# A recurrence with two expert layers on one core: the bonus moves onto the diagonal of the scores, the state products go into 64-row quarters, and the first product takes tokens as its stationary operand

## The chip, the cores and the metric

The kernel runs on one core of a Trainium2 chip. The metric is the device time of one execution in microseconds (us). The inputs lie in the chip's main memory, `w_in` and `w_out` of the first layer as float64, the others as float32, and the float32 output is written there.

## The reference

Three parts follow one another. The first is a recurrence over time for 4 batches of 8 heads, 768 steps, head size 48. The second and the third are layers on the 3072 tokens that it gives, each a vector of 384.

```python
# recurrence, per batch and head; u is the bonus of the present step
for t in range(S):
    cur = outer(u * k[t], v[t])
    y[t] = r[t] @ (state + cur)
    state = w[t][:, None] * state + outer(k[t], v[t])
# first layer: x is y as [3072, 384]
h = x @ w_in                    # [3072, 2048]
g = h * cos(h)
x = g @ w_out                   # [3072, 384]
# second layer: 8 experts with 4 slots each
logits = x @ phi                # [3072, 32]
slots = softmax(logits, over tokens).T @ x
slot_out = relu(slots @ w1[e]) @ w2[e]      # for each expert e
out = softmax(logits, over slots) @ slot_out
```

## The kernel before

The recurrence is cut into 24 blocks `j` of 128 tokens (six to a batch), and each block into two chunks `c` of 64. Within a chunk the decays become running products by two scans on VectorE (`scan`, `sp`; lines 156 and 164), and the recurrence becomes small products for four pairs of heads. Step `A` (line 208) gives the scores of each chunk, key by query. Step `mask` (line 222) multiplies them by a strict triangle of ones, from PSUM into the tile `L`. The other half of `L` holds the decayed `r` (step `L`, line 187). Step `U` (line 259) adds up the chunk's own contribution to the state, `st` and `z` (lines 277 and 269) carry the state on, and `y` (line 288) multiplies `L` by a tile `rzs` that holds both the state and `v`.

The bonus `u` of the present step goes another way. `ru` on GpSimd (lines 169 and 170) multiplies `r`, `u` and `k`, `bo` on VectorE (line 243) sums that over a head, `bv` on GpSimd (line 251) multiplies the sum by `v`, and `yb` (line 297) adds it to `y` in PSUM with three transposing matmuls. From block 8 on (`WIDE = 8`) the matmuls of `A` take all 128 rows, half of them zeros, for which GpSimd clears half of `L` (`zl`, line 193). In `U` the operand `vz` has `v` of chunk 0 in its upper 64 rows and of chunk 1 in its lower, side by side with zeros, so that one matmul gives both chunks (96 columns).

The first layer works in 12 groups `g` of 256 tokens and 8 pairs `i` of 128 features each. `h` (lines 462 to 464) has weights as the stationary operand (`lhsT`) and tokens as the moving one, 18 matmuls of 256 columns for a pair, since both are split into a rounded and a remaining part. `turns`, `rest`, `cos` and `mul` (lines 474, 478, 482, 486) make `g` out of it on ScalarE and VectorE in turn. `l` (line 507) makes logits from `g`, `gT` and `gc` (lines 494, 499) turn `g` so that tokens lie on partitions, and `E` (line 603) sums up the slots from that. The product with `w_out` is folded into `phi` and into the slots; at the start the weights are decoded to float32 from the 64-bit words of the float64 inputs, on ScalarE and VectorE (`raw`, `abs`, `mx`, `d1`, `d2a`, `d2b`; lines 338 to 374), and `w_in` is split into its two parts (`whi`, `wn`, `wc`; line 405 is the second half of `wn`).

The order is written out by hand. A string `HEAD` lists some 2,000 steps with their block or group, and each engine takes its instructions in that order. All DMAs are issued from SP. Transposes, `A`, `U`, `y`, `wn` and some others get their PSUM from one pool `ps_a` of three banks, `h` from a pool of two.

Of the kernel before, what the change touches and what calls it, by code (L numbers as in the profile page):

```python
# [21 lines left out]
def rwkv_moe_kernel(ctx: ExitStack, tc: tile.TileContext, r, k, v, w, u, w_in, w_out, phi, w1, w2, cst, out):  # L22
# [7 lines left out]
    C = 64  # L30
# [6 lines left out]
    NBK = MF // 2  # L37
# [5 lines left out]
    WIDE = 8  # L43
# [10 lines left out]
    g_p = b_stack.enter_context(tc.tile_pool(name="g", bufs=4, side="right"))  # L54
    gt_p = b_stack.enter_context(tc.tile_pool(name="gt", bufs=12, side="right"))
# [35 lines left out]
    vz = [nat.tile([128, H, 2, D], F32, name=f"vz{i}") for i in range(2)]  # L91
# [14 lines left out]
    vn_t, rz_t, l_t, ks_t, ksn_t, q_t, bv_t, z_t = ({} for _ in range(8))  # L106
# [60 lines left out]
    def e_ru(j):  # L167
# [3 lines left out]
        bv_t[j] = ru  # L171
# [30 lines left out]
    def e_A(j):  # L202
        ks, L = ks_t[j], l_t[j]
# [68 lines left out]
    def e_rz(j, c):  # L272
        for a in range(2):
            nc.scalar.copy(rz_t[j][64 * a:64 * a + 64, c, :, a, RZ[a]], z_t[j, c][64 * a:64 * a + 64])  # L274

    def e_st(j, c):
        nc.vector.tensor_tensor(out=st_state, in0=pend["U", j][:, :, c, :], in1=z_t[j, c], op=ALU.add)

    def e_y(j):

        L, rz = l_t.pop(j), rz_t.pop(j)
        ps = tps(f"y{j}")[:, 0:DM].rearrange("p (c t) -> p c t", c=KD)
        begun = set()
# [66 lines left out]
    def e_abs(x, n, hf=None):  # L350
        if not hf:
# [94 lines left out]
    LAST = (NG - 1, NBK - 1)  # L446

    def b_h(g, i, mm):
        if mm == 0:
            pool, tag = (ps_a, "a") if NBK * g + i >= ATT else (ps_h, "h")  # L450
            hp = pool.tile([128, 2, G], F32, tag=tag, name=f"h{g}_{i}")
            h_t[g, i] = [hp[:, 0], hp[:, 1], hp]
        elif (g, i) == LAST:
            h_t[g, i][1] = ps_t.tile([128, 2, G], F32, tag="t", name=f"h{g}_{i}b")[:, 0]
        hp = h_t[g, i][mm]
        xh, xl = xh_t[g], xl_t[g]
        m = 2 * i + mm
# [611 lines left out]
```

## Time and profile before

| | |
|---|---|
| time, median of 3 runs | 543.63 us (542.59 to 544.12) |
| profiled execution: span from first to last instruction | 542.5 us |
| TensorE (PE) busy | 502.9 us, 93% |
| VectorE (DVE) busy | 435.2 us, 80% |
| ScalarE (ACT) busy | 310.7 us, 57% |
| GpSimd (POOL) busy | 125.4 us, 23% |
| mean granted TensorE clock | 0.98 of full speed |

The span is taken from one execution by the profiler; what lies around it (1.1 us to the median) is start and end of the program. Busy time is an average over stages with different limits, and matmuls overlap, so PE's busy time is no sum of their durations.

### The profile page before, as it was taken

How to read it: one execution, taken by the hardware profiler on the slowest of the kernel's cores; microseconds unless marked ns; L12 is line 12 of the kernel's file. 1: busy time of each engine (PE TensorE's matmuls, PEld its weight loads, DVE VectorE, ACT ScalarE, POOL GpSimd, SP SyncE). 2: the span in 40 equal slices, each digit the busy share in tenths (PEclk: the TensorE clock that was granted, in tenths of full speed). 3: DMA queues.
4: the chain of work that ended last, by engine and by line, in shares of the span. 5: the costliest groups of instructions: out<-in, count | busy, mean ns of one | idle time of the engine just before them, and what ended most of it. 6: DMA issues, size and time to landing. Idle time of an engine off the chain costs nothing.

```text
span 542.5 us, 16245 instructions
## 1 busy us (share of the span) xinstructions
PE 502.9 (93%) x6850; PEld 436.4 (80%) x6850; DVE 435.2 (80%) x826; ACT 310.7 (57%) x655; POOL 125.4 (23%) x163
## 2 busy tenths in 40 slices
PE   2769879989999999999999999999999999998994
PEld 1547668879898898999988989989998989894673
DVE  4999998998889879887879788989878877666423
ACT  3356567646747555676555665755657646666421
POOL 4520120254044213221420331352033100000400
PEclk9977998999999999999999999999999999999998
DMA  9994656444332432421440442065031565188958
GB/s 218 258 238 105 176 115 183 125 76 75 74 59 46 76 59 50 79 37 30 76 74 1 75 89 45 17 111 83 16 61 31 229 252 220 29 322 311 403 181 272
DMA packets 146713, 67.52 MB, mean 124 GB/s; under 512 B 127569, under 2 KB 134737, under 8 KB 146641
## 3 DMA queue, kind: packets, MB, share of 16 engines
q1 hardware_dynamic: 146640, 66.49, 48.4%
q8 instruction: 54, 0.88, 0.7%
q14 instruction: 19, 0.15, 0.1%
HBM read 61.75 MB, written 4.72 MB: 123 GB/s over the span
## 4 chain that ended last, share of the span: by engine, by line
PE 67%; DVE 18%; ACT 5%; DMA 4%; issue 2%; SPq 2%; DVEq 0%; ACTq 0%
PE h L462 10%; PE h L464 10%; PE h L463 10%; PE gT L494 6%; PE l L507 4%; PE E L603 3%; PE A L208 3%; PE y L288 3%; PE U L259 2%; DMA vz<-in_v_dram 2%; PE hps L797 2%; DMA rawi<-in_moe_w_in_dram 2%; PE so L837 2%; DVE L L222 2%; DVE pt L164 2%
## 5 line engine op out<-in xcount | busy, mean ns | idle before, releaser
L462 PE MATMUL h<-x,wu 128*128 128x256 f32 x573 | 171.5, 299 | 1.4 <-DVE g L486 1.3
L464 PE MATMUL h<-x,wu 128*128 128x256 f32 x573 | 160.9, 281 | 0.0
L463 PE MATMUL h<-x,wu 128*128 128x256 f32 x573 | 160.8, 281 | 0.0
L462 PEld LDWEIGHTS h<-x,wu 128*128 128x128 f32 x573 | 108.7, 190 | 3.6 <-DVE g L486 1.7
L463 PEld LDWEIGHTS h<-x,wu 128*128 128x128 f32 x573 | 108.8, 190 | 0.2
L464 PEld LDWEIGHTS h<-x,wu 128*128 128x128 f32 x573 | 108.5, 189 | 0.0
L482 ACT ACTIVATE g<-g,half_pi 128x512 f32<-128x512 f32 (+1 forms) x97 | 69.4, 719 | 44.7 <-DVE g L478 43.7
L486 DVE TENSOR_TENSOR g<-g,h 128x512 f32<-128x512 f32 x96 | 64.8, 677 | 26.7 <-ACT g L482 26.1
L474 ACT ACTIVATE g<-h 128x512 int32<-128x512 f32 x96 | 57.1, 596 | 42.0 <-PE h L464 32.6
L478 DVE SCALAR_TENSOR_TENSOR g<-g,h 128x512 f32<-128x512 int32 x96 | 65.0, 678 | 14.9 <-ACT g L474 13.9
L251 POOL TENSOR_TENSOR bv<-vz,bo 64x384 f32<-64x384 f32 x48 | 43.8, 914 | 139.5 <-DVE bo L243 54.6
L499 ACT COPY gt<-gT 128x512 f32<-128x512 f32 x89 | 51.6, 584 | 28.7 <-PE gT L494 28.1
L494 PE MATMUL gT<-cs,g 128*128 128x128 f32 x384 | 58.1, 275 | 0.3 <-ACT gt L499 0.2
L494 PEld LDWEIGHTS gT<-cs,g 128*128 128x128 f32 x384 | 43.7, 140 | 6.0 <-issue 3.7
L169 POOL TENSOR_TENSOR ru<-rn,u_b 128x384 f32<-128x384 f32 x24 | 27.5, 1145 | 57.2 <-issue 19.5
L193 POOL MEMSET L<- 64x512 f32 x32 | 16.6, 520 | 96.0 <-PE y L288 81.5
L156 DVE TENSOR_TENSOR_SCAN qt<-wf,one_b 128x520 f32<-128x520 f32 x24 | 30.6, 1275 | 7.3 <-ACT wf L151 7.3
L222 DVE TENSOR_TENSOR L<-A,cs 64x512 f32<-64x512 f32 x48 | 33.0, 688 | 4.0 <-PE A L208 2.9
L274 ACT COPY rzs<-z 64x192 f32<-64x192 f32 x96 | 33.4, 348 | 3.6 <-DVE z L269 2.6
L187 DVE TENSOR_TENSOR L<-rT,pt 64x512 f32<-64x512 f32 x48 | 32.9, 686 | 1.6 <-PE rT L141 0.6
L164 DVE TENSOR_TENSOR_SCAN pt<-wf,ini_f 128x520 f32<-128x520 f32 x24 | 31.7, 1320 | 0.1
L208 PE MATMUL A<-L,ks 128*64 128x64 f32 (+1 forms) x768 | 27.7, 223 | 3.2 <-DVE ks L199 2.1
(172 smaller groups left out, 837.8 us busy)
## 6 DMA issues: line engine op xcount, KB each, us to landing
we<-in_moe_w_dram SPq DMA_DIRECT2D x16, 1536.0 KB, 10.4
rawi<-in_moe_w_in_dram SPq DMA_DIRECT2D x7, 768.0 KB, 5.5
wn<-in_w_dram SPq DMA_DIRECT2D x24, 192.0 KB, 4.0
kn<-in_k_dram SPq DMA_DIRECT2D x24, 192.0 KB, 4.0
rn<-in_r_dram SPq DMA_DIRECT2D x24, 192.0 KB, 3.8
vz<-in_v_dram SPq DMA_DIRECT2D x48, 96.0 KB, 3.1
rzs<-in_v_dram SPq DMA_DIRECT2D x96, 48.0 KB, 2.8
out_dram<-ob SPq DMA_DIRECT2D x17, 256.0 KB, 3.6
```

The costliest lines, as they stand in the source:

```text
L208: nc.tensor.matmul(ps[64 - 64 * a:128 - 64 * a, s, :], lhsT=ks[k, s, :], rhs=L[k, a, s, :], start=True, stop=True)
L222: nc.vector.tensor_tensor(out=L[h, a], in0=ps[h], in1=mask[h].unsqueeze(1).to_broadcast([64, NS, C]), op=ALU.mult)
L251: nc.gpsimd.tensor_tensor(out=bv[h], in0=vn_t[j][h, :, c, :], in1=bo[h].to_broadcast([64, H, D]), op=ALU.mult)
L462: nc.tensor.matmul(hp, lhsT=wh, rhs=xh[:, c, :], start=(c == 0), stop=False)
L463: nc.tensor.matmul(hp, lhsT=wh, rhs=xl[:, c, :], start=False, stop=False)
L464: nc.tensor.matmul(hp, lhsT=wl, rhs=xh[:, c, :], start=False, stop=(c == KD - 1))
L474: nc.scalar.activation(gt.bitcast(I32), hp, AF.Copy, bias=0.25, scale=1.0 / TWO_PI)
L478: nc.vector.scalar_tensor_tensor(out=gt, in0=gt.bitcast(I32), scalar=-TWO_PI, in1=hp, op0=ALU.mult, op1=ALU.add)
L482: nc.scalar.activation(gt, gt, AF.Sin, bias=half_pi[:, 0:1])
L486: nc.vector.tensor_tensor(out=gt, in0=gt, in1=hp, op=ALU.mult)
L494: nc.tensor.transpose(ps[:, tt, mm, :], gt[:, mm, tt * 128:(tt + 1) * 128], ident)
L499: (nc.vector.tensor_copy if NBK * g + i >= ATT and i in (1, 2, 5) else nc.scalar.copy)(t, pend.pop(("gT", g, i)))
```

## The change

The bonus sum is written onto the diagonal of the scores. `bo` writes its sums beside each other, a new step `bs` copies the half that belongs to other partitions (two small copies on ScalarE), and a new step `D` on GpSimd writes the diagonal with zeros elsewhere into the scores' half of the tile (`affine_select`, two of 64x512 a block). `mask` then copies the scores over it only where the triangle is one (`copy_predicated` on VectorE). `bv`, `yb`, `zl` and their tiles are gone, and `A` takes 64 rows in every block. `U` is made of 16 matmuls of 48 columns in place of 8 of 96, each with 64 rows and 64 columns of the array, chunk 0 and chunk 1 into PSUM banks of their own; `v` comes by one DMA a block, not two.

In the first layer `x` becomes the stationary operand and the weights the moving one: 9 matmuls of 512 columns for 128 tokens and 512 features (`b_h`), 96 times. So `g` has tokens on partitions. `E` reads `g` itself (512 columns a matmul), `l` reads the turned copy (128 columns a matmul, 384 of them in place of 192 of 256). The pool of `g` grows from 4 to 13 buffers, that of the turned copies shrinks from 12 to 3. `HEAD` is a new list.

```diff
-    NBK = MF // 2
+    NBK = 4
+    NGB = 13
-    WIDE = 8
...
-    g_p = b_stack.enter_context(tc.tile_pool(name="g", bufs=4, side="right"))
-    gt_p = b_stack.enter_context(tc.tile_pool(name="gt", bufs=12, side="right"))
+    g_p = b_stack.enter_context(tc.tile_pool(name="g", bufs=NGB, side="right"))
+    gt_p = b_stack.enter_context(tc.tile_pool(name="gt", bufs=16 - NGB, side="right"))
...
     def e_A(j):
...
-                k = slice(0, 128) if j >= WIDE else slice(64 * a, 64 * a + 64)
+                k = slice(64 * a, 64 * a + 64)
...
-    def e_mask(j):
-        L, ps = l_t[j], pend.pop(("A", j))
+    def e_D(j):
+
         for a in range(2):
             h = slice(64 - 64 * a, 128 - 64 * a)
-            nc.vector.tensor_tensor(out=L[h, a], in0=ps[h], in1=mask[h].unsqueeze(1).to_broadcast([64, NS, C]), op=ALU.mult)
+            nc.gpsimd.affine_select(out=lt[j % 2][h, a], in_=bo_t[j][h, a].unsqueeze(2).to_broadcast([64, NS, C]),
+                                    pattern=[[0, NS], [-1, C]], compare_op=ALU.is_equal, fill=0.0, base=0, channel_multiplier=1)
+
+    def e_mask(j):
+        ps = pend.pop(("A", j))
+        for a in range(2):
+            h = slice(64 - 64 * a, 128 - 64 * a)
+            nc.vector.copy_predicated(out=lt[j % 2][h, a], mask=mask[h].bitcast(U32).unsqueeze(1).to_broadcast([64, NS, C]), data=ps[h])
...
+    def e_bs(j):
+        bo = bo_t[j]
+        for a in range(2):
+            nc.scalar.copy(bo[64 - 64 * a:128 - 64 * a, a, a::2], bo[64 * a:64 * a + 64, a, 1 - a::2])
...
     def e_U(j):
-        ksn, vn = ksn_t.pop(j), vn_t[j]
-        ps = tps(f"U{j}")[:, 0:2 * HP * D].rearrange("p (s c d) -> p s c d", c=2, d=D)
+        ksn = ksn_t.pop(j)
+        ps = [tps(f"U{j}_{c}")[:, 0:HP * D].rearrange("p (s d) -> p s d", d=D) for c in range(2)]
         for p in range(HP):
             for a in range(2):
-                nc.tensor.matmul(ps[64 * a:64 * a + 64, p], lhsT=ksn[:, p * 128 + 64 * a:p * 128 + 64 * a + 64],
-                                 rhs=vn[:, 2 * p + a], start=True, stop=True)
+                for c in range(2):
+                    h = slice(64 * c, 64 * c + 64)
+                    nc.tensor.matmul(ps[c][64 * a:64 * a + 64, p], lhsT=ksn[h, p * 128 + 64 * a:p * 128 + 64 * a + 64], rhs=vn[j % 2][h, 2 * p + a], start=True, stop=True)
...
-    def e_yb(j):
-
-        y = bv_t.pop(j).rearrange("p h d -> p (h d)")
-        for c in range(KD):
-            nc.tensor.matmul(pend["xT", j][:, c, :], lhsT=y[:, c * 128:(c + 1) * 128], rhs=ident, is_transpose=True,
-                             start=False, stop=c == KD - 1, skip_group_check=True)
...
+        o = (t % 2) * TB
+        xh, xl = (x[:, :, o:o + TB] for x in (xh_t[t // 2], xl_t[t // 2]))
+        for half, f in zip(h_t[t, q], cols):
+            for c in range(KD):
+                wh, wl = wu[q][:, 0, c, f], wu[q][:, 1, c, f]
+                nc.tensor.matmul(half[:, f], lhsT=xh[:, c, :], rhs=wh, start=(c == 0), stop=False)
+                nc.tensor.matmul(half[:, f], lhsT=xl[:, c, :], rhs=wh, start=False, stop=False)
+                nc.tensor.matmul(half[:, f], lhsT=xh[:, c, :], rhs=wl, start=False, stop=(c == KD - 1))
...
-            nc.tensor.matmul(lps_t[g][32 * mm:32 * mm + 32, 0:G], lhsT=p_sb[:, m, :], rhs=g_t[g, m // 2][:, m % 2, :],
-                             start=(m < 4), stop=(m >= MF - 4))
+            nc.tensor.matmul(lps_t[g][32 * m:32 * m + 32, o:o + TB], lhsT=p_sb[:, 4 * q + m, :], rhs=gt[:, m * 128:(m + 1) * 128],
+                             start=first, stop=False, skip_group_check=True)
...
-                                 rhs=gt_t[g, 4 * hf + q][:, tt, :], start=(tt == 0), stop=(tt == 1))
+                nc.tensor.matmul(ps[32 * q:32 * q + 32, cols], lhsT=dt_[:, tt, :], rhs=g_t[2 * g + tt, q][:, cols], start=(tt == 0), stop=(tt == 1))
```

The order of the instructions shows at three places what moved. A row has the line, the operation, output and inputs with their buffers, the output's shape and a count. The first place is TensorE at block 13, before the change: `U` and the scores `A` of the block, two steps of `l`, and `y` with the bonus product of the block before.

```order
L259 MATMUL U_3710<-vz_124,ksn_3642 64x96 x8
L208 MATMUL A_3719<-L_3689,ks_3590 64x64 x16
L507 MATMUL l_3499<-g_4_3619,p_sb 32x256 x2
L507 MATMUL l_3499<-g_5_3565,p_sb 32x256 x2
L288 MATMUL y_3747<-L_3330,rzs_125 32x64 x32
L297 MATMUL y_3747<-cs,bv_3413 128x128 x3
```

After the change, at block 14, `A` is followed by 16 matmuls of `U`, by turns into its two banks. Here are the last two of them and what comes behind.

```order
L239 MATMUL U_0_3766<-vn_123,ksn_3728 64x48
L239 MATMUL U_1_3767<-vn_123,ksn_3728 64x48
L468 MATMUL gT_2_3806<-cs,g_2_3726 128x128 x4
L434 MATMUL h_0_3811<-wu_345,x_3054 128x512
L435 MATMUL h_0_3811<-wu_345,x_3054 128x512
L436 MATMUL h_0_3811<-wu_345,x_3054 128x512
```

Between `U` and the next step that needs a bank of `ps_a` now stand a transposition of `g` and a product `h`; line 297 is gone. The second place is GpSimd at the first two blocks, before the change: `ru` for both, then `bv` for both.

```order
L169 TENSOR_TENSOR ru_201<-rn_117,u_b 128x384
L170 TENSOR_TENSOR ru_201<-ru_201,kn_119 128x384
L169 TENSOR_TENSOR ru_249<-rn_118,u_b 128x384
L170 TENSOR_TENSOR ru_249<-ru_249,kn_120 128x384
L251 TENSOR_TENSOR bv_354<-vz_123,bo_238 64x384 x2
L251 TENSOR_TENSOR bv_487<-vz_124,bo_288 64x384 x2
```

After the change the diagonal of a block stands behind its own `ru` and ahead of the next block's.

```order
L162 TENSOR_TENSOR ru_195<-rn_117,u_b 128x384
L163 TENSOR_TENSOR ru_195<-ru_195,kn_119 128x384
L207 AFFINE_SELECT lt_125<-bo_217 64x512 x2
L162 TENSOR_TENSOR ru_282<-rn_118,u_b 128x384
L163 TENSOR_TENSOR ru_282<-ru_282,kn_120 128x384
L207 AFFINE_SELECT lt_126<-bo_303 64x512 x2
```

So GpSimd reaches `ru` of block 1 only when `D` of block 0 has had its sums. The third place is VectorE at block 0, before the change, from the sum `bo` of block 0 to that of block 1.

```order
L243 TENSOR_REDUCE bo_238<-ru_201 128x8
L160 RECIPROCAL ini_f<-qt_215 128x8
L366 SCALAR_TENSOR_TENSOR ai_187<-rawi_185,ai_187 128x3x128
L164 SCALAR_TENSOR_TENSOR pt_247<-wf,ini_f 128x520
L187 TENSOR_TENSOR L_254<-rT_226,pt_247 64x512 x2
L222 TENSOR_TENSOR L_196<-A_264,cs 64x512 x2
L243 TENSOR_REDUCE bo_288<-ru_249 128x8
```

After the change, from `L` of block 0 to the masked copy and `ks` of block 1.

```order
L178 TENSOR_TENSOR lt_125<-rT_179,pt_192 64x512 x2
L225 TENSOR_REDUCE bo_217<-ru_195 128x2x4
L149 SCALAR_TENSOR_TENSOR qt_243<-wf,one_b 128x520
L256 TENSOR_TENSOR st_state<-U_0_223,z_0_163 128x192
L153 RECIPROCAL ini_f<-qt_243 128x8
L248 TENSOR_TENSOR z_1_273<-st_state,qt_189 128x192
L214 COPY_PREDICATED lt_125<-cs,A_246 64x512 x2
L184 TENSOR_TENSOR ks_280<-kT_268,qt_243 128x512
```

The masked copy of block 0 stands five instructions behind the sum `bo` of that block, on which it now depends by way of ScalarE and GpSimd; before, nothing on VectorE waited for that sum.

## Rows read from the trace of the kernel before

**Rows 1.** Page of the profile, part 1: busy us, share of the span, instructions of each engine.

```profile
PE 502.9 (93%) x6850; PEld 436.4 (80%) x6850; DVE 435.2 (80%) x826; ACT 310.7 (57%) x655; POOL 125.4 (23%) x163
```

**Rows 2.** Stretch, length, busy us of PE, PEld, DVE, ACT, POOL (xinstructions), PEclk, DMA share, GB/s.

```profile
0.00:120.00 120.00, 93.14 (x1078) 74.72 (x1079) 107.85 (x166) 66.41 (x128) 32.30 (x48) 0.93 0.73 169
120.00:490.00 370.00, 365.80 (x5085) 331.94 (x5083) 306.67 (x610) 224.45 (x478) 86.43 (x106) 1.00 0.37 85
490.00:543.00 53.00, 43.92 (x689) 29.73 (x689) 20.71 (x52) 19.86 (x50) 6.68 (x10) 0.95 0.84 297
```

**Rows 3.** Who TensorE waited for, 120 to 490 us: total us, times, longest.

```profile
PE kN L215 <- DVE ini_f L160: 1.3, 1, 1.3
```

**Rows 4.** Who VectorE waited for, 120 to 490 us: total us, times, longest.

```profile
DVE g L486 <- ACT g L482: 26.4, 40, 1.3
```

**Rows 5.** Line 462 alone, every third matmul of `h`, 120 to 490 us: PE busy (xcount).

```profile
120.00:490.00 370.00, 155.05 (x519) 98.39 (x519) 1.00 0.37 85
```

**Rows 6.** TensorE in order of time, 300.8 to 304.4: start us, us, line, xcount.

```profile
300.53 0.49 PE L297 MATMUL y<-cs,bv 128*128 128x128 f32 x3
300.86 0.60 PE L215 MATMUL kN<-cs,ks 128*128 128x128 f32 x4
...
301.65 0.36 PE L462 MATMUL h<-x,wu 128*128 128x256 f32 x1
301.86 0.28 PE L463 MATMUL h<-x,wu 128*128 128x256 f32 x1
...
303.88 0.60 PE L494 MATMUL gT<-cs,g 128*128 128x128 f32 x4
```

**Rows 7.** TensorE in order of time, 86 to 89.5 us.

```profile
86.06 0.60 PE L404 MATMUL wl<-ai,cs 128*128 128x256 f32 x2
86.31 0.47 PE L405 MATMUL wl<-wu,neg 128*128 128x256 f32 x1
86.61 1.02 PE L404 MATMUL wl<-ai,cs 128*128 128x512 f32 x2
87.07 0.79 PE L405 MATMUL wl<-wu,neg 128*128 128x512 f32 x1
```

**Rows 8.** TensorE in order of time, 334 to 336.3 us.

```profile
333.76 0.64 PE L507 MATMUL l<-g,p_sb 128*32 128x256 f32 x8
334.33 0.88 PE L259 MATMUL U<-vz,ksn 128*64 128x96 f32 x16
335.04 1.10 PE L208 MATMUL A<-L,ks 128*64 128x64 f32 x32
336.07 0.44 PE L494 MATMUL gT<-cs,g 128*128 128x128 f32 x2
```

**Rows 9.** TensorE in order of time, 256 to 259 us.

```profile
257.88 1.08 PE L288 MATMUL y<-L,rzs 128*32 128x64 f32 x64
258.89 0.33 PE L297 MATMUL y<-cs,bv 128*128 128x128 f32 x1
```

**Rows 10.** Line 297, the bonus product, before 120 us.

```profile
0.00:120.00 120.00, 2.55 (x12) 1.43 (x12) 0.93 0.73 169
```

**Rows 11.** Line 259, the product `U`, after 120 us.

```profile
120.00:490.00 370.00, 15.66 (x288) 12.49 (x288) 1.00 0.37 85
```

**Rows 12.** Groups by line and form: busy us, mean ns of one, idle before, releaser.

```profile
L251 POOL TENSOR_TENSOR bv<-vz,bo 64x384 f32<-64x384 f32 x48 | 43.8, 914 | 139.5 <-DVE bo L243 54.6 <-PE kN L215 22.4 <-DMA kn<-in_k_dram 15.4
...
L222 DVE TENSOR_TENSOR L<-A,cs 64x512 f32<-64x512 f32 x48 | 33.0, 688 | 4.0 <-PE A L208 2.9
...
L156 DVE TENSOR_TENSOR_SCAN qt<-wf,one_b 128x520 f32<-128x520 f32 x24 | 30.6, 1275 | 7.3 <-ACT wf L151 7.3
...
L193 POOL MEMSET L<- 64x512 f32 x32 | 16.6, 520 | 96.0 <-PE y L288 81.5 <-issue 13.6
...
L277 DVE TENSOR_TENSOR st_state<-U,z 128x192 f32<-128x192 f32 x48 | 16.5, 344 | 1.8 <-PE U L259 1.3
...
L541 ACT COPY dl<-lc 32x64 f32<-32x64 f32 x48 | 9.7, 201 | 3.4 <-DVE mx L530 2.9
```

More of the change, by code (lines that the diff above doesn't have):

```diff
@@ L103, in segs @@
         return t[:, lo:lo + NS * SEG].rearrange("p (s j) -> p s j", j=SEG)[:, :, 0:n]
-    vn_t, rz_t, l_t, ks_t, ksn_t, q_t, bv_t, z_t = ({} for _ in range(8))
+    ks_t, ksn_t, q_t, ru_t, bo_t, z_t = ({} for _ in range(6))
     xh_t, xl_t = {}, {}
@@ L350, in e_abs @@
     def e_abs(x, n, hf=None):
-        if not hf:
+        if (x, n) not in a_t:
             a_t[x, n] = dec.tile([128, 768], F32, tag="a", name=f"a{x}{n}")
@@ L444, in rwkv_moe_kernel @@
     g_t, gt_t, lps_t, h_t = {}, {}, {}, {}
[L446 to L457, printed above, removed]
-        o = (m % 4) * 128
-        wt = wu[m // 4]
-        for c in range(KD):
-            wh, wl = wt[:, 0, c, o:o + 128], wt[:, 1, c, o:o + 128]
-            nc.tensor.matmul(hp, lhsT=wh, rhs=xh[:, c, :], start=(c == 0), stop=False)
-            nc.tensor.matmul(hp, lhsT=wh, rhs=xl[:, c, :], start=False, stop=False)
-            nc.tensor.matmul(hp, lhsT=wl, rhs=xh[:, c, :], start=False, stop=(c == KD - 1))
@@ L474, in b_turns, with bank, b_rest @@
+    def bank(t, q, hf):
+        if hf is None:
+            return g_t[t, q], h_t[t, q][0]
+        f = slice(hf * 256, hf * 256 + 256)
+        return g_t[t, q][:, f], h_t[t, q][hf][:, f]
+    def b_turns(t, q, hf=None):
+        if (t, q) not in g_t:
+            g_t[t, q] = g_p.tile([128, 512], F32, tag="g", name=f"g{t}_{q}")
+        gt, hp = bank(t, q, hf)
         nc.scalar.activation(gt.bitcast(I32), hp, AF.Copy, bias=0.25, scale=1.0 / TWO_PI)
-    def b_rest(g, i, mm=None):
-        gt, hp = bank(g, i, mm)
+    def b_rest(t, q, hf=None):
+        gt, hp = bank(t, q, hf)
@@ L510, in rwkv_moe_kernel, with b_t, b_tc @@
-    sm, e_ps = {}, {}
+    def b_t(t, q):
+        gt = g_t[t, q]
+        pool, tag = (ps_h, "h") if NBK * t + q >= ATT else (ps_t, "t")
+        ps = pool.tile([128, 512], F32, tag=tag, name=f"gT{t}_{q}")
+        for m in range(4):
+            nc.tensor.transpose(ps[:, m * 128:(m + 1) * 128], gt[:, m * 128:(m + 1) * 128], ident)
+        pend["gT", t, q] = ps
+    def b_tc(t, q):
+        gt_t[t, q] = gt_p.tile([128, 512], F32, tag="gt", name=f"gt{t}_{q}")
+        n = NBK * t + q
+        (nc.vector.tensor_copy if n >= ATT and n % 8 in (1, 2, 5) else nc.scalar.copy)(gt_t[t, q], pend.pop(("gT", t, q)))
@@ L512, in s_sum, with b_l @@
+    def b_l(t, q):
+        g, first = t // 2, t // 2 not in lps_t
+        if first:
+            lps_t[g] = ps_l.tile([128, 512], F32, tag="l", name=f"l{g}")
+        o, gt = (t % 2) * TB, gt_t.pop((t, q))
+        for m in range(4):
+            nc.tensor.matmul(lps_t[g][32 * m:32 * m + 32, o:o + TB], lhsT=p_sb[:, 4 * q + m, :], rhs=gt[:, m * 128:(m + 1) * 128],
+                             start=first, stop=False, skip_group_check=True)
+    sm, e_ps, lcp, dt_s = {}, {}, {}, {}
     def s_sum(g):
@@ L655, in rwkv_moe_kernel @@
             nc.gpsimd.memset(t[:, :, D:C], 1.0)
-        for c in range(2):
-            for t in vz:
-                nc.gpsimd.memset(t[64 * c:64 * c + 64, :, 1 - c, :], 0.0)
         for t in rzs:
@@ new lines @@
+l.5.2 l.5.3 mul.6.0 sum.2 ru.12 rz.10.0 U.10 A.10 rest.6.3 cos.6.3 st.10.0 bo.12 kT.11 z.10.1 mul.6.3 lc.2 max.2 exp.2 xt.2 gT.6.1 h.6.2 xr.2
+turns.6.2 mask.10 xd.2 rz.9.0 h.7.1 rT.11 gc.6.1 rest.6.2 st.10.1 turns.7.1 dT.2 scan.12 ltok.2 gT.6.0 ru.11 y.9 dc.2 sr.12 gc.6.0 cos.6.2 rest.7.1
+l.6.0 mul.6.2 L.11 E.2.0 bo.11 ks.11 l.6.1 cos.7.1 xh.9 gT.6.2 mul.7.1 h.7.0 lv.11 z.11.0 xl.9 gc.6.2 turns.7.0 kN.11 lk.13 rest.7.0 cos.7.0 gT.6.3
+lz.10 h.7.3 ksn.11 U.11 A.11 gc.6.3 mul.7.0 turns.7.3 cmb.0.0 st.11.0 lz.11 lw.14 bs.11 rest.7.3 cos.7.3 D.11 gT.7.1 rz.10.1 h.7.2 sp.12 kT.12 gc.7.1
@@ L1019 @@
+mul.23.3.0 gc.23.1 gT.23.3 l.23.1 gc.23.3 l.23.2 l.23.3 sum.11 lc.11 we.7 E.10.1 tab max.11 quart.11 exp.11 dT.11 es.10 dc.11 E.11.1 E.11.0 esl.11.1
+ltok.11 esl.11.0
 """
```

320 lines of the change are left out of this document (128 added, 192 removed).

## The prediction

> **What bounds the kernel now.** I read the page's busy times first, then the same by stretches, then the waits, then TensorE in order of time. The page puts TensorE at 93% and VectorE at 80% [rows 1], but that is a mean over three stages [rows 2]. Up to 120 us VectorE is busy for 107.85 us of 120 and TensorE for 93.14: there the weights are decoded, and VectorE is the bound. From 120 to 490 us TensorE is busy for 365.80 us of 370 and VectorE for 306.67 (83%); the longest of the five waits that TensorE has there is 1.3 us [rows 3], while VectorE's first one in the list, 26.4 us in 40 times, is for ScalarE inside the chain that makes `g` [rows 4]. So this stage is as long as TensorE's instructions make it, and each microsecond taken from them is worth about one, until VectorE binds. The last 53 us hold the second layer, whose matmuls and weights the change leaves alone. The sum is therefore made for 120 to 490 us, where 519 matmuls of line 462 stand [rows 5]; with the other two lines that is 3 x 519 / 18 = 86.5 of 96 blocks of `h`.
>
> The span is 542.5 us, 1.1 us less than the median of 543.63 us; I take the change off the median.
>
> **The change part by part, on TensorE.** *First product.* A run of 18 matmuls of 256 columns starts at 301.65 us, and the next step at 303.88: 2.23 us [rows 6]. The first takes 0.21 us to the second, the 17 others 2.02 us, 0.119 us each. So the start of a run costs 0.09 us, and a matmul 0.119 us, which at the 2.4 GHz of that stage (granted clock 1.00 [rows 2]) are 286 cycles for 256 columns. What the other 30 cycles hang on decides the price of 512 columns. If they go with the columns, it is 0.238 us, and nothing is gained. If they belong to the matmul, it is 542 cycles, 0.226 us. If a longer matmul hides them, it is 0.213 us. A row of this kernel has such a matmul, line 405: the pair of line 404 before it ends at 86.61 + 1.02 = 87.63 us, it ends at 87.07 + 0.79 = 87.86, so 0.23 us, against 86.78 - 86.66 = 0.12 us for 256 columns [rows 7]. That is nearest to 0.226 us, which I take: 9 x 0.226 + 0.09 = 2.12 us for a block, 0.11 us less, x 86.5 = -9.5 us. The bounds are 0 and -19 us (2.01 us a block). Runs of `h` also become fewer, 117 before and 91 after by the two lists of TensorE's instructions: 26 x 0.09 = -2.3 us.
>
> The Trainium skill (TensorE: Matmul & The Clock Gate, Back-to-back issue gap) puts the warm distance of two matmuls at columns / 2.4 ns + 2.5 ns, which is an estimate of 0.109 us for 256 columns and 0.216 us for 512. By it alone the first product would gain 2 us, not 9.5, and the whole would come to 535 us. The row of 0.119 us does not agree with it for 256 columns, and no row here tells for a stream of 512.
>
> *Bonus product.* It takes 300.86 - 300.53 = 0.33 us a block [rows 6]; 12 of its 72 matmuls, 4 blocks, lie before 120 us [rows 10], so 20 x 0.33 = -6.6 us.
>
> *State product.* `U` takes 335.04 - 334.33 = 0.71 us [rows 8], and 288 / 16 = 18 of them lie after 120 us [rows 11]. Its 16 passes become 32 of 48 columns. If they run two at a time as those of `A` do (32 passes of 64 columns, 1.03 us [rows 8]), they take 1.03 x 48 / 64 = 0.77 us. If four at a time, as the four column groups of `y` (64 passes of 64 columns in 1.01 us [rows 9]), they take 1.01 / 2 x 48 / 64 = 0.38 us. Four matmuls that follow each other now use four different quarters, as four of `y` use four groups, so I lean to that: 0.45 us, 18 x 0.26 = -4.7 us, bounds -6 and +1 us.
>
> *Logits and slots.* `l` and `E` keep their columns, and the transpositions their number. `l` comes in 54 runs for 38, and by the start cost above that is 16 x 0.09 = +1.4 us; I take +2 (0 to +4).
>
> Together -9.5 - 2.3 - 6.6 - 4.7 + 2 = -21.1 us.
>
> **What lies beside it.** The masked copy on VectorE has no row. The product that it replaces took 0.688 us for 64x512 [rows 12]; the slowest row of that length is the scan, 1275 ns for 520 columns, 1.26 us for 512. Like the product it reads one operand from PSUM and one from SBUF and goes through each element once, so I take 0.69 us, no change. `D` on GpSimd lies between the clearing (520 ns) and the two-input product (914 x 512 / 384 = 1.22 us) [rows 12]: 25 to 58 us in all, where `bv` and the clearing took 43.8 + 16.6. GpSimd is idle for three quarters of the time, so that costs nothing unless somebody waits. `bs` adds 48 copies like the 201 ns row of line 541 [rows 12], some 10 us on ScalarE, busy for 224 us of 370 [rows 2]; behind it in ScalarE's queue stand the steps that make `g`, each late by 0.4 us once a block if that cover goes. `v` comes by half as many DMAs with the same bytes: nothing, since no DMA is among the waits of TensorE or VectorE in the middle stage.
>
> One wait is added: the masked copy now needs `bo`, then `bs`, then `D`. Block 0 has four other VectorE instructions between sum and copy, a scan among them, some 2 us; the way through `bs` and two of `D` takes 0.4 + 1.0 to 2.4 us. VectorE may stand still for a microsecond in some of the first blocks, and all its decoding behind that; I take 0 and keep +3 us for the range. Later the chain is far ahead.
>
> With 21 us less, VectorE's 306.7 us stand in 349 us, 88% for 83%, and `U` holds two of three banks. Some of the gain will come back as short waits: I choose +5 us. It is no more than a choice; five waits so far came to under 3 us. So 543.6 - 21.1 + 5 = **527.5 us**, 3% faster.
>
> **The rivals.** *Banks (slower).* `U` holds two of the pool's three banks until VectorE has done `st`, `z`, `st` (`st` 344 ns each [rows 12]), which may stand behind other work of 0.7 us or more. If the next transposition or `A` comes first, TensorE stops with all of `h` queued behind it, and the masked copy, `ks` and `L` come late too. From 0.9 us a block (21.1 / 24) the gain is gone; at 1.5 us it is 543.6 - 21 + 36 = 558 us. For it speaks that the stage has no slack on TensorE, against it that one bank hardly caused a wait [rows 3] and that the new list often puts a transposition of `g` or a whole `h`, 2 us, behind `U`. Chance 0.12. The Trainium skill (TensorEngine Tiling (Array Packing), Gotcha 1: PSUM Pressure) says that different row tiles must write different banks, so that the pressure on PSUM grows with row tiling; by that rule the second bank can't be avoided, and no run here shows it.
>
> *VectorE takes over (no gain).* If the masked copy goes at the scan's rate, each costs 0.57 us more. Six of 24 blocks have their `U` before 120 us [rows 11], where VectorE binds; with two copies each that is +6.8 us. The other 36 put it at 327 of 349 us, 94%, and I count half of their 20.5 us: 527.5 + 17 = 544 us. Chance 0.10, half of it within the noise.
>
> *No gain in `h`.* With 0.238 us for 512 columns the whole is 527.5 + 9.5 = 537 us. Chance 0.13.
>
> *All of it.* With 0.213 us, `U` at 0.38 us, `l` free and nothing given back: 19 + 2.3 + 6.6 + 6 = 34 us, 510 us. Chance 0.13.
>
> **How the numbers follow.** My forecast, 518 to 536 us by its own bounds, has 0.52. What a measurement of this kernel can tell from no change is about 0.3%. Faster are the forecast, the third and the fourth rival: 0.78. Half of the second is within 0.3%: 0.05. The rest, 0.17, is slower. The range leaves out the banks (0.12) and the far end of the fourth: 509 to 545 us.
>
> **What would show it.** Right: runs of 9 in `h` at 0.22 to 0.23 us a matmul, `U` under 0.5 us, no line 297's successor, the masked copy near 0.69 us, TensorE busy throughout from 120 us, the last `h` some 16 us earlier, and the first stage as long as now. Wrong: TensorE waiting for `st` behind a transposition or `A` (banks); the masked copy at 1.2 us and VectorE with no idle time; VectorE waiting for GpSimd's diagonal; `U` in pairs at 0.77 us; `h` at 0.238 us; or a first stage of another length, since a new list can start `h` sooner or later than the old one.

## The result, and the profile after

The changed kernel takes 528.93 us (median of 4 runs, 527.60 to 529.87); the kernel before took 543.88 us beside it (4 runs, 542.59 to 544.86). The ratio is 0.972, with a 95% interval of 0.970 to 0.975: 2.8% faster, 15 us. The forecast was 527.5 us. The profiled execution has a span of 528.2 us.

The page of the changed kernel, part 1, which answers to [rows 1]:

```profile
PE 486.2 (92%) x6515; PEld 381.2 (72%) x6515; DVE 434.1 (82%) x826; ACT 319.4 (60%) x703; POOL 100.0 (19%) x127
```

The same by stretches, as [rows 2]; the second layer now begins some 16 us earlier, so the cuts lie at 475 and 529:

```profile
0.00:120.00 120.00, 93.43 (x1166) 71.31 (x1167) 109.00 (x171) 70.67 (x146) 32.02 (x47) 0.89 0.73 172
120.00:475.00 355.00, 351.05 (x4688) 281.46 (x4688) 305.20 (x608) 230.75 (x512) 61.30 (x70) 1.00 0.38 88
475.00:529.00 54.00, 41.67 (x665) 28.48 (x663) 19.88 (x49) 18.00 (x46) 6.67 (x10) 0.95 0.82 289
```

The first stretch still belongs to VectorE (109.00 us of 120). In the middle TensorE is busy for 351.05 us of 355, so it is still the bound there, and VectorE has come up to 86%. The last `h` starts at 470.8 us where it started at 487.9, 17 us earlier; about 16 were forecast. Not all of that reaches the end: the first product of the experts (`hps`, lines 797 and 767) starts at 489.0 us where it started at 503.5, 14.5 us earlier. Between the last `h` and it the changed kernel takes 2.6 us more, in `l`, `dT` and `E` and in waits for VectorE and ScalarE. The forecast left the last 53 us out of its sum.

What TensorE waited for from 120 to 475 us, complete, as [rows 3] (total us, times, longest):

```profile
PE l L483 <- ACT gt L474: 1.6, 1, 1.6
PE h L434 <- DVE g L461: 0.8, 2, 0.4
PE E L579 <- ACT dt L560: 0.5, 2, 0.3
PE gT L468 <- ACT gt L474: 0.5, 1, 0.5
PE E L579 <- DVE ltok L566: 0.3, 1, 0.3
PE rT L134 <- PE h L436: 0.2, 1, 0.2
```

Together 3.9 us, none for `st` (the banks of `U`) and none for `mask`. Ahead of 120 us there are such waits:

```profile
PE wl L376 <- DVE lt L214: 3.5, 2, 2.2
PE wl L376 <- DVE st_state L256: 0.9, 2, 0.5
PE y L267 <- DVE st_state L256: 0.7, 1, 0.7
PE kT L134 <- DVE st_state L256: 0.5, 1, 0.5
```

That is 2.1 us for `st`, 0.9 in the kernel before, and 3.5 for the masked copy, 0.2 before. TensorE's idle time in the first 120 us is the same in all, 120 - 93.43 = 26.6 us for 26.9, so nothing shows that they cost time. A block of `h` in order of time (start, duration of one; `...` leaves out five matmuls), as [rows 6]:

```profile
300.75 0.50 PE L434 MATMUL h<-wu,x 128*128 128x512 f32 x1
301.09 0.39 PE L435 MATMUL h<-wu,x 128*128 128x512 f32 x1
301.32 0.40 PE L436 MATMUL h<-wu,x 128*128 128x512 f32 x1
...
302.70 0.40 PE L436 MATMUL h<-wu,x 128*128 128x512 f32 x1
302.94 0.27 PE L553 MATMUL dT<-cs,dl 128*128 128x128 f32 x1
303.68 0.66 PE L468 MATMUL gT<-cs,g 128*128 128x128 f32 x4 [0.48 <-ACT gt L474]
```

From the second matmul to the ninth, seven steps take 302.70 - 301.09 = 1.61 us, 0.230 us each, and the block 302.94 - 300.75 = 2.19 us. The last row shows a small give-back: after `dT` TensorE stands 0.48 us because `gT` waits for ScalarE's copy `gt`, which empties the one PSUM bank that `gT` has. `A` and `U` beside each other, as [rows 8]:

```profile
333.93 0.59 PE L496 MATMUL lc<-lg,cs 128*128 128x256 f32 x2
334.45 0.97 PE L193 MATMUL A<-lt,ks 64*64 64x64 f32 x26
335.21 0.25 PE L239 MATMUL U<-vn,ksn 64*64 64x48 f32 x1
335.25 0.23 PE L193 MATMUL A<-lt,ks 64*64 64x64 f32 x2
...
335.43 0.62 PE L239 MATMUL U<-vn,ksn 64*64 64x48 f32 x28
335.98 0.66 PE L468 MATMUL gT<-cs,g 128*128 128x128 f32 x4
```

The last passes of `A` and the first of `U` interleave; both together take 335.98 - 334.45 = 1.53 us, where [rows 8] has 336.07 - 334.33 = 1.74 us. The new steps beside TensorE, over the whole kernel (busy us, mean ns of one, idle before):

```profile
L214 DVE COPY_PREDICATED lt<-cs,A 64x512 f32<-64x512 uint32 x48 | 35.4, 737 | 3.2 <-PE A L193 1.8
L207 POOL TENSOR_SCALAR_AFFINE_SELECT lt<-bo 64x512 f32<-64x512 f32 x48 | 35.3, 736 | 179.6 <-ACT bo L230 121.3 <-PE y L267 15.9 <-issue 15.8
...
L230 ACT COPY bo<-bo 64x4 f32<-64x4 f32 x48 | 9.3, 193 | 3.4 <-DVE bo L225 2.3
```

VectorE's masked copy waited for the scores (1.8 us in all), and GpSimd's diagonals are named nowhere as what it waited for.

**Where the time came from.** For every matmul of the two traces I took the time from its start to the start of the next one on TensorE, which holds the waits too, and summed that by step from 120 us to the end. In us (the last row holds all steps, also those not listed):

| step | before | after | difference | forecast |
|---|---|---|---|---|
| `h` | 197.2 | 187.4 | -9.8 | -11.8 |
| bonus product | 6.5 | 0 | -6.5 | -6.6 |
| `U` | 13.9 | 10.7 | -3.2 | -4.7 |
| `A` | 19.1 | 17.7 | -1.5 | 0 |
| `l` | 24.2 | 25.7 | +1.6 | +2 |
| `dT`, `E`, `wT` | 30.5 | 35.0 | +4.5 | in the give-back, +5 |
| all steps | 414.6 | 400.1 | -14.5 | -16.1 |

The two sums do not hold quite the same work: after the change 0.9 block of `h` and one `y` more lie before 120 us, some 3 us. `y` itself has 19.5 us before and 19.4 after, for one block fewer, because the 1.6 us that `l` waits for `gt` follow a `y` and are counted there.

### The profile page after: what moved, and what is told of

Same layout as the page of the kernel before. It is cut to its first block, busy times and chain, and to the rows that moved or that the text cites. A ratio compares the mean times of both kernels' runs of the same rounds, so it can differ in the third digit from the quotient of the medians.

```text
span 528.2 us, 15546 instructions
## 1 busy us (share of the span) xinstructions
PE 486.2 (92%) x6515; PEld 381.2 (72%) x6515; DVE 434.1 (82%) x826; ACT 319.4 (60%) x703; POOL 100.0 (19%) x127
## 4 chain that ended last, share of the span: by engine, by line
PE 70%; DVE 18%; ACT 4%; DMA 4%; issue 2%; SPq 0%; ACTq 0%; DVEq 0%
PE h L434 11%; PE h L436 10%; PE h L435 10%; PE gT L468 7%; PE l L483 4%; PE E L579 4%; PE y L267 4%; PE A L193 3%; PE U L239 2%; PE hps L767 2%; DVE lt L214 2%; PE so L807 2%; PE wT L134 2%; PE kT L134 2%; PE kN L200 1%
## 5 line engine op out<-in xcount | busy, mean ns | idle before, releaser
L434 PE MATMUL h<-wu,x 128*128 128x512 f32 x288 | 121.6, 422 | 0.8 <-DVE g L461 0.8
L436 PE MATMUL h<-wu,x 128*128 128x512 f32 x288 | 113.1, 393 | 0.0
L435 PE MATMUL h<-wu,x 128*128 128x512 f32 x288 | 112.5, 391 | 0.0
L449 ACT ACTIVATE g<-h 128x512 int32<-128x512 f32 (+1 forms) x96 | 57.1, 596 | 54.4 <-PE h L436 47.2
L453 DVE SCALAR_TENSOR_TENSOR g<-g,h 128x512 f32<-128x512 int32 (+1 forms) x96 | 64.6, 675 | 12.2 <-ACT g L449 11.7
L207 POOL TENSOR_SCALAR_AFFINE_SELECT lt<-bo 64x512 f32<-64x512 f32 x48 | 35.3, 736 | 179.6 <-ACT bo L230 121.3
L434 PEld LDWEIGHTS h<-wu,x 128*128 128x128 f32 x288 | 54.2, 188 | 15.0 <-DVE g L461 4.1
L436 PEld LDWEIGHTS h<-wu,x 128*128 128x128 f32 x288 | 54.0, 188 | 12.4
L435 PEld LDWEIGHTS h<-wu,x 128*128 128x128 f32 x288 | 54.4, 189 | 8.7
L162 POOL TENSOR_TENSOR ru<-rn,u_b 128x384 f32<-128x384 f32 x24 | 28.9, 1203 | 137.5 <-DVE bo L225 70.3
L214 DVE COPY_PREDICATED lt<-cs,A 64x512 f32<-64x512 uint32 x48 | 35.4, 737 | 3.2 <-PE A L193 1.8
L483 PE MATMUL l<-gt,p_sb 128*32 128x128 f32 x768 | 31.7, 277 | 1.9 <-ACT gt L474 1.6
L178 DVE TENSOR_TENSOR lt<-rT,pt 64x512 f32<-64x512 f32 x48 | 32.8, 684 | 0.5
L267 PEld LDWEIGHTS y<-lt,rzs 128*32 128x32 f32 x1536 | 24.7, 112 | 6.3 <-issue 2.4
```

What stands on the lines that cost most here:

```text
L214: nc.vector.copy_predicated(out=lt[j % 2][h, a], mask=mask[h].bitcast(U32).unsqueeze(1).to_broadcast([64, NS, C]), data=ps[h])
L434: nc.tensor.matmul(half[:, f], lhsT=xh[:, c, :], rhs=wh, start=(c == 0), stop=False)
L435: nc.tensor.matmul(half[:, f], lhsT=xl[:, c, :], rhs=wh, start=False, stop=False)
L436: nc.tensor.matmul(half[:, f], lhsT=xh[:, c, :], rhs=wl, start=False, stop=(c == KD - 1))
L449: nc.scalar.activation(gt.bitcast(I32), hp, AF.Copy, bias=0.25, scale=1.0 / TWO_PI)
L453: nc.vector.scalar_tensor_tensor(out=gt, in0=gt.bitcast(I32), scalar=-TWO_PI, in1=hp, op0=ALU.mult, op1=ALU.add)
```

## The experiments

In all of them TensorE's steps are summed as above, from 120 us on, against the changed kernel. Differences in time to the changed kernel are made by ratios to the kernel before, which ran beside each.

**U in pairs.** The chunk becomes the outermost loop of `U`, so that four matmuls that follow each other use two quarters, not four.

```diff
-        for p in range(HP):
-            for a in range(2):
-                for c in range(2):
+        for c in range(2):
+            for p in range(HP):
+                for a in range(2):
```

> The changed kernel with one edit: in U the chunk is the outermost loop, so that matmuls that follow each other use two quarters by turns and not four. Same matmuls, banks and list. Theory (the quarters run four at a time): U goes from about 0.5 us to the 0.77 us of two at a time, 0.26 us for each of the 18 to 20 blocks in the stage that TensorE bounds, so 4.7 to 5.2 us more than the changed kernel's 528.9 us: 533.5 to 534.5 us, ratio to before 0.981. Rival (the time of U hangs on the number of passes, not on which quarters follow each other): 529 us, ratio 0.972.

Measured: 533.38 us, ratio 0.982 (0.979 to 0.984), 1.0% or 5 us slower. `A` and `U` in order of time:

```profile
337.56 0.97 PE L193 MATMUL A<-lt,ks 64*64 64x64 f32 x26
...
338.53 0.91 PE L239 MATMUL U<-vn,ksn 64*64 64x48 f32 x29
339.37 0.66 PE L468 MATMUL gT<-cs,g 128*128 128x128 f32 x4
```

The same step, behind the same `lc`, takes 339.37 - 337.56 = 1.81 us instead of 1.53, and the sum of `U` rises by 4.3 us. Nothing but the order of the 16 matmuls of `U` (32 passes) differs, so the quarters do run four at a time, as the forecast leaned to.

**U whole.** `U` as before the change (8 matmuls of 96 columns over 128 rows, which are 16 passes; zeros beside `v`, two loads a block, one bank), all else as changed. The edit of `U`:

```diff
-                for c in range(2):
-                    h = slice(64 * c, 64 * c + 64)
-                    nc.tensor.matmul(ps[c][64 * a:64 * a + 64, p], lhsT=ksn[h, p * 128 + 64 * a:p * 128 + 64 * a + 64], rhs=vn[j % 2][h, 2 * p + a], start=True, stop=True)
+                nc.tensor.matmul(ps[64 * a:64 * a + 64, p], lhsT=ksn[:, p * 128 + 64 * a:p * 128 + 64 * a + 64],
+                                 rhs=vn[:, 2 * p + a], start=True, stop=True)
```

> The changed kernel with U as before: v beside zeros, 8 matmuls of 96 columns over 128 rows, one bank, two DMAs a block. Theory (the quarters are worth what TensorE saves): U goes from about 0.5 us back to 0.71 us, 0.2 us in 18 to 20 blocks, about 4 us: 533 us, ratio 0.980. Rival (the second bank takes the gain back by waits): with one bank the kernel is as fast or faster, 525 to 529 us, ratio 0.965 to 0.972.

Measured: 535.61 us, ratio 0.985 (0.983 to 0.987), 1.3% or 7 us slower. TensorE in order of time:

```profile
329.82 0.88 PE L244 MATMUL U<-vz,ksn 128*64 128x96 f32 x16
330.63 1.15 PE L199 MATMUL A<-lt,ks 64*64 64x64 f32 x32
331.71 0.86 PE L489 MATMUL l<-gt,p_sb 128*32 128x128 f32 x24
```

`U` takes 0.81 us here and `A` 1.08, and so they do in each of the 15 blocks where they adjoin: 1.89 us together. In the kernel before, where both used 128 rows and 64 columns, [rows 8] has 0.71 and 1.03. Where they do not adjoin, they take 0.81 and 1.08 us in the kernel before too (7 blocks each). So a part of the gain comes from the neighbourhood: two steps that cut the array in the same way take 0.15 us less side by side (1.74 for 1.89), two that cut it differently do not. The Trainium skill (TensorEngine Tiling (Array Packing), Key Properties) says that a change of tiling mode, not of the tile alone, drains TensorE; this trace agrees, with those 0.15 us a pair. The sums rose by 3.9 us for `U`, 1.8 for `A` and 1.2 for `h`. The theory's 4 us are those of `U` alone. The rival, banks, fell: with one bank nothing became faster.

**h in halves.** Each matmul of `h` is made as two of 256 columns, tokens stationary as in the changed kernel.

```diff
-        cols = [slice(0, 512)]
-        h_t[t, q] = [hp]
+        cols = [slice(0, 256), slice(256, 512)]
+        h_t[t, q] = [hp, hp]
...
```

> The changed kernel with each matmul of the first product cut into two of 256 columns, 18 to a block as before, x still stationary, same list. Theory (a part of a matmul's time hangs on the matmul and not on its columns): a block takes 18 x 0.119 + 0.09 = 2.23 us instead of the 2.18 us that the trace of the changed kernel shows, and by the interval sums of both traces up to 0.11 us more; over 87 blocks 4 to 10 us: 533 to 539 us, ratio 0.980 to 0.991. Rival (what was gained in h is the fewer runs and the other orientation, not the long matmuls): 529 us, ratio 0.972.

Measured: 538.01 us, ratio 0.990 (0.987 to 0.992), 1.8% or 9.5 us slower. A block in order of time (`...` leaves out 16 of its 18 matmuls):

```profile
302.38 0.37 PE L433 MATMUL h<-wu,x 128*128 128x256 f32 x1
302.58 0.28 PE L434 MATMUL h<-wu,x 128*128 128x256 f32 x1
...
304.70 1.15 PE L193 MATMUL A<-lt,ks 64*64 64x64 f32 x32
```

The block takes 304.70 - 302.38 = 2.32 us, the median of those that stand alone is 2.24, against 2.18 in the changed kernel and 2.23 in the kernel before, where the weights were stationary. `h` accounts for 7.1 us of the loss, of which 1.6 are 0.7 block that here lies behind 120 us; `y` (+1.9) and `A` (+0.7) make up the rest. So the matmuls' length is worth 5.5 us at equal work, and which operand is stationary changes nothing that shows.

**Zeros behind y.** Three transposing matmuls of a tile of zeros follow each `y`. In the kernel before the bonus product stood directly behind a `y` in only 5 of the 20 blocks after 120 us.

```diff
+        for o in range(KD):
+            nc.tensor.matmul(ps[:, o, :], lhsT=zero_t, rhs=ident, is_transpose=True, start=False, stop=o == KD - 1, skip_group_check=True)
...
```

> The changed kernel with three more transposing matmuls behind each y, of a tile of zeros, which add nothing to the result: the TensorE work of the old bonus product and nothing else of it. Theory (each microsecond of TensorE in the middle stage is worth one): 0.33 us in 20 blocks, 6.6 us: 535.5 us, ratio 0.984. Rival (the product was hidden behind waits, and its removal gave nothing): 529 us, ratio 0.972.

Measured: 540.01 us, ratio 0.993 (0.991 to 0.996), 2.2% or 11.5 us slower. TensorE in order of time:

```profile
257.40 1.08 PE L268 MATMUL y<-lt,rzs 128*32 128x64 f32 x64
258.40 0.55 PE L272 MATMUL y<-cs,zero_t 128*128 128x128 f32 x3
258.88 0.43 PE L486 MATMUL l<-gt,p_sb 128*32 128x128 f32 x8
```

The three take 0.48 us here (median of 19 blocks 0.48, sum 9.5 us with a wait of 1.1), and `y` before them is longer by 0.8 us in sum. The bonus product took 0.33 us [rows 6]. The direction is as expected, the size is not, and the starts in the two traces show why: it is the place, not the zeros. The first transpose takes 0.165 us to the next where `y` or `l` stands before it, which cut the array into 128x32, and 0.109 behind a step over the whole array. The last takes 0.203 us ahead of a step that cuts the array, 0.109 ahead of one over the whole array and 0.03 ahead of `h`. Here all 19 stand behind `y`, and 14 of them ahead of `l` or `E` (128x32); in the kernel before 9 of 20 stood behind `y` or `l`, and 2 ahead of a step that cuts the array. The gain that belongs to the change is therefore the 6.5 us of the table, not these 11.5.

**No diagonal.** The steps `D` leave the list, and the tiles are cleared once; the bonus is left out, its sum and copies stay.

```diff
+        for t in lt:
+            for a in range(2):
+                nc.gpsimd.memset(t[64 - 64 * a:128 - 64 * a, a], 0.0)
...
```

> The changed kernel without the steps D: the scores' half of the two tiles is cleared once at the start and the masked copy goes into zeros. It leaves out the bonus. The bonus sum, its copy and all else stay where they are. Theory (the chain from the bonus sum over the two ScalarE copies to the diagonal is early enough everywhere, so it costs nothing): 528 to 530 us, within 0.3% of the changed kernel, and the masked copies wait as before for the scores alone. Rival (the masked copies on VectorE wait for GpSimd's diagonals, above all in the first 120 us where VectorE is the bound): 3 to 6 us faster, 523 to 526 us.

Measured: 527.18 us, ratio 0.968 (0.967 to 0.970), 0.4% or 2 us faster; the interval just touches the changed kernel's (0.970 to 0.975). In the traces the last `h` starts at 469.9 us against 470.8. The first stretch:

```profile
0.00:120.00 120.00, 92.43 (x1171) 70.39 (x1172) 109.60 (x173) 71.78 (x148) 25.66 (x40) 0.96 0.73 172
```

VectorE has two more instructions behind it at 120 us than in the changed kernel (173 for 171). So the diagonals cost 1 to 2 us, in the traces all of it in the first stage. That is just outside the theory's 528 to 530 us, and the rival's 3 to 6 us are not there; what the sums and the two copies cost was not measured.

**The bonus alone, in the old list.** The kernel before, with the bonus on the diagonal and nothing else of the change. I put the product, the bonus sum, the copies and `D` into the old list by a rule (the copies 4 steps behind the sum), and left the other steps where they were.

```diff
+            nc.gpsimd.affine_select(out=lt[j % 2][h, a], in_=bo_t[j][h, a].unsqueeze(2).to_broadcast([64, NS, C]),
+                                    pattern=[[0, NS], [-1, C]], compare_op=ALU.is_equal, fill=0.0, base=0, channel_multiplier=1)
...
-            nc.vector.tensor_tensor(out=L[h, a], in0=ps[h], in1=mask[h].unsqueeze(1).to_broadcast([64, NS, C]), op=ALU.mult)
+            nc.vector.copy_predicated(out=lt[j % 2][h, a], mask=mask[h].bitcast(U32).unsqueeze(1).to_broadcast([64, NS, C]), data=ps[h])
...
-    def e_yb(j):
...
```

> The kernel before with its old list, in which only the bonus moves: bonus sums, copies and diagonals in place of the product with v and of the three transposes behind y; scores of 64 rows in every block; no clearing of zeros by GpSimd. U stays whole, the first product stays with weights stationary. Theory (the three transposes cost about 0.43 us a block behind y, 20 blocks after 120 us, so 8 to 9 us, some of which comes back as waits since the list was not made for it): 535 to 538 us, ratio 0.985 to 0.99. Rival 1 (their price is the 0.33 us that the trace of before shows as the run's own length): 537 to 539 us. Rival 2 (the list puts the masked copy, which is longer by 0.05 us, or the chain to the diagonal, in TensorE's way): 542 us or more.

Measured: 555.15 us, ratio 1.020 (1.018 to 1.022), 10.7 us slower. I had expected a gain; this is rival 2. TensorE did lose the 6.5 us of the bonus product, but other steps took longer by more. ScalarE's waits over the whole kernel (total, times, longest):

```profile
ACT bo L240 <- DVE bo L234: 13.2, 9, 3.4
```

Here ScalarE stands 13.2 us for the bonus sum, with the steps of `g` queued behind it, and from 123 us on TensorE's `h` took 4.7 us longer, `gT` 3.7 and `l` 1.5 than in the kernel before from 120 us on, at equal counts of matmuls. Much of that is idle time: the list of TensorE's waits from 120 us to the last `h` adds up to 11.1 us here and to 2.7 in the kernel before, and up to 120 us TensorE is idle for 31.3 us, not 26.9.

**The same with more distance.** The ScalarE copies stand 21 steps behind the bonus sum, and the bonus product directly behind its operands' loads; block 12 in the list, as an example of the 24:

```diff
- ru.12, 141 places on bo.12, 5 on bs.12, 1 on D.12, 34 on mask.12
+ ru.12, 156 places on bo.12, 21 on bs.12, 1 on D.12, 15 on mask.12
```

> As the kernel before with the bonus alone (which was 10.7 us slower), but with more steps of the list between the links of the chain: the bonus product as early as its operands allow, the two ScalarE copies 21 steps behind the bonus sum instead of 4. Theory (in the first version ScalarE, which takes its instructions in order, waited 13.2 us in 9 places for the bonus sum, and g behind it came late): ScalarE's wait for the bonus sum goes under 3 us and the time falls to 538 to 547 us, since TensorE has 6.5 us less to do and only the other shifts of the list stay. Rival (the slower time is the work itself, as the masked copy or the diagonals): it stays within 3 us of 555 us.

Measured: 550.39 us, ratio 1.011 (1.010 to 1.013): 0.8% or 4.6 us better than the first version, still 6 us worse than the kernel before. ScalarE's wait for the sum is no longer among its ten longest, and another has grown, on VectorE (0.4 us in the first version), since the same edit leaves `D` 15 places ahead of the masked copy instead of 34:

```profile
DVE lt L215 <- POOL lt L222: 2.9, 4, 1.2
```

So the distance explains less than half of the loss; neither the theory's 538 to 547 us nor the rival's 552 to 558 us is met. Of the rest, some 1.1 us are `A` and `U`, which no longer cut the array in the same way (33.0 us before, 34.1 here). TensorE's waits from 120 us to the last `h` still add up to 8.7 us, the largest sum of them for the last step of `g` on VectorE (over the whole kernel):

```profile
PE h L443 <- DVE g L467: 2.3, 6, 1.0
```

What makes that step late stays open.

**The distance taken away in the new list.** In 19 blocks of the changed kernel the copies go back to 4 steps behind the bonus sum; block 12 as an example:

```diff
- bo.12, 98 places on bs.12, 35 on D.12
+ bo.12, 4 places on bs.12, 129 on D.12
```

> The changed kernel with the two ScalarE copies moved back to 4 steps behind the bonus sum in the 19 blocks in which they are farther; nothing else. Theory (the chain costs nothing only because of the distance that the new list gives it): ScalarE waits some 5 to 13 us for the bonus sum and the time is 531 to 537 us. Rival (TensorE's order hides such waits in this list, as ScalarE is free a third of the time): 528 to 530 us.

Measured: 531.46 us, ratio 0.976 (0.974 to 0.978), 0.4% or 2 us slower, with the last `h` 2.7 us later in the traces; by the times alone the two intervals overlap (0.970 to 0.975 for the changed kernel). ScalarE's waits:

```profile
ACT bo L230 <- DVE bo L225: 11.4, 8, 2.9
```

They were 2.3 us in the changed kernel. Theory right, at the lower end: the chain is cheap because of its distance, and without that it costs 2 to 3 us more.

**Maxima on GpSimd.** All 17 `mx` steps of the decoding, or only the 8 of `w_out`, move from VectorE to GpSimd.

```diff
-                "mx": e_mx, "mxp": lambda x, n: e_mx(x, n, eng=nc.gpsimd),
+                "mx": e_mx, "mxp": lambda x, n, hf=None: e_mx(x, n, hf, eng=nc.gpsimd),
...
- mx.i.2
+ mxp.i.2
...
```

> The changed kernel with all 17 maximum steps of the decoding of the weights on GpSimd in place of VectorE, in the same places of the list. Theory (until about 120 us VectorE is the bound, TensorE waits for it there and not after): the 17 steps of some 0.55 us leave VectorE, the 9th product's end at 118 us comes up to 9 us earlier, and 520 to 526 us follow. Rival (each such step stands behind the diagonals and the bonus products in GpSimd's queue and takes longer there, so that the decoding itself becomes late): 528 to 534 us.

> As the kernel with all 17 maximum steps on GpSimd, but only the 8 of w_out, which the first product doesn't wait for. Theory (VectorE's work in the first 120 us is what counts, whatever it is): up to 4.4 us faster than the changed kernel, 524.5 to 527.5 us. Rival (the first stage is set by the chain of one step behind the other, not by VectorE's sum): no change, 528 to 530 us.

Measured: 541.70 us (ratio 0.995, 0.994 to 0.996) and 535.22 us (0.984, 0.982 to 0.986), 2.3% and 1.2% slower than the changed kernel. VectorE's own steps in the changed kernel, first 120 us:

```profile
L329 DVE TENSOR_SCALAR ao<-ao 128x768 f32<-128x768 f32 x8 | 4.4, 552 | 1.3 <-ACT ao L325 1.3
```

The same on GpSimd, in the kernel with eight moved, and what VectorE then waited for in the first 125 us:

```profile
L329 POOL TENSOR_SCALAR ao<-ao 128x768 f32<-128x768 f32 x8 | 18.7, 2333 | 20.2 <-ACT ao L325 19.2 <-POOL lt L207 1.0
```

```profile
DVE ao L333 <- POOL ao L329: 5.4, 4, 2.0
```

A step of 552 ns becomes one of 2333 ns, and VectorE, freed of 4.4 us, waits 5.4 us for it. Both theories fell. The first rival was right in the mechanism (the steps take longer there, and the decoding becomes late) and too mild in the size; the second, that nothing would change, was not met either. Whether a shorter VectorE would shorten the first stage was not told apart, because its steps became a wait on it.

No experiment that keeps the bonus gave a kernel faster than the changed one. What the new order of the list gives by itself is not told apart: no run has it without the changed steps, and `h` with tokens stationary was not run in the old list.

## Why the prediction was right, step by step

- **What bounds it.** Right: TensorE from 120 us, 351.05 us of 355, and of the 19.4 us by which `h`, the bonus product, `U`, `A` and `l` together became shorter (forecast: 21.1), 14.5 came through. The first stage was not quite "as long as now": TensorE gets some 3 us more of the work done in it, in the same busy time (93.43 us for 93.14), which the forecast had at nothing.
- **h.** The direction is right, and the main term was mis-sized: the length of the matmuls gave 5.5 us where 9.5 were forecast. A matmul of 512 columns takes 0.230 us, not 0.226 (542 cycles was the right kind of price, slightly low, and the row of line 405, 0.23 us [rows 7], was the better value), and a block takes 2.18 us for 2.12. By block, `h` went from 197.2 / 86.5 = 2.28 to 187.4 / 85.6 = 2.19 us (85.6 blocks: 770 matmuls of 9 to a block), which is -7.8 us where -11.8 was forecast. The other 2 us of the table's -9.8 are 0.9 block that now lies before 120 us. The halves part the -7.8: as many runs as after the change, but matmuls of 256 columns, gave 2.25 us a block, so 2.2 us are the fewer runs (-2.3 forecast) and 5.5 the length. The Trainium skill (TensorE: Matmul & The Clock Gate, Back-to-back issue gap) has 0.216 us for 512 columns as the gap of an isolated matmul and about 0.131 us for a stream with a weight load for each; these traces agree with neither, with 0.230 for 512 and 0.119 for 256.
- **Bonus product.** -6.5 us for -6.6. That the change removes it is shown; but the two versions in the old list show that taking it away gains nothing where the chain that replaces it is badly placed.
- **U.** Four quarters at a time, as chosen: shown by the pairs. The sum of -4.7 us is exact, by luck in its parts: `U` alone gave 3.2 us, and `A`, which the forecast left out, 1.5, because the two now overlap where they adjoin. The 0.71 us of [rows 8] holds only where `A` follows; the mean of the 18 blocks was 0.77 and is now 0.59. Where `U` stands alone it takes 0.61 us (0.81 before), not under 0.5.
- **l and the give-back.** +1.6 us for +2; and +4.5 us in `dT`, `E` and `wT` with 0.4 in small ones, for the +5 that was "no more than a choice": that the size fits is luck. Where it would show was not forecast: a part is `gT` waiting for its bank behind `dT` (0.48 us in the row above), a cause that the row names and no experiment took away, and 1.5 us of the 4.5 stand behind the last `h`.
- **What lies beside it.** The masked copy takes 737 ns (0.69 forecast), 2.4 us more for VectorE in all. `D` takes 736 ns, within 0.52 to 1.22 us; `bs` 193 ns for about 0.2 us. Nearly all hidden, as said: the diagonals cost 1 to 2 us, inside the 0 to 3 that the range kept.
- **The rivals.** Banks: no wait for `st` on TensorE from 120 us on, 2.1 us ahead of that, and the version with one bank was slower. That `U` needs two was not tested; the 64-row tiles of `A` write the two halves of one. VectorE taking over: the masked copy is nowhere near 1.26 us, VectorE has 86%. No gain in `h`, and all of it: 0.230 us lies between 0.213 and 0.238, so neither.

## What to carry to other kernels

When a stage is bound by TensorE's instructions alone, sum the time from each start to the next by step: such sums foretold this change within 2 us, in part by luck: `h` gave 4 us less at equal work, the first stage some 3 us that the forecast had not counted, and the give-back was a guess. Prefer long streams and quarter tiles that follow each other in different quarters, and put steps that cut the array in the same way side by side. Work moved to idle engines is cheap only as far as the order leaves distance between its links, so move the order together with the work.

## What the runs showed of the hardware that was not expected

- `A` and `U` take 1.89 us when one uses 64x64 and the other 128x64 tiles, 1.74 us when both use 128x64, and 1.53 us in the same 64x64 tiles side by side, where their passes interleave.
- Three transposes over the whole array take 0.33 us beside steps over the whole array [rows 6] and 0.48 us between `y` and `l`, which cut it into 128x32.
- A maximum with a constant over 128x768 takes 2333 ns on GpSimd and 552 ns on VectorE, 4.2 times as long. The Trainium skill (GPSIMD Engine Reference, Engine selection) puts operations with one input roughly at line rate there; these rows do not agree.
- The mean granted clock of the first 120 us, a mixture of TensorE's two levels, was 0.89 in the changed kernel and 0.96 without the diagonals, and the last `h` started only 0.9 us apart: in this pair of traces TensorE's clock hardly showed in a stretch that VectorE fills.
